# Five reloads on a second queue: which queue starts the first loads of pass two of a scaling kernel

## The chip, the cores and the metric

One core of one Trainium2 chip. In this kernel TensorE sums the pixels, ScalarE helps to pack them and computes the sigmoid, VectorE scales and unpacks, SyncE only starts transfers, and 16 DMA engines move the data between DRAM and SBUF, the core's memory on chip. The metric is the device time of one execution in microseconds; a kernel's time is the median of several. The kernel before took 723.08 us (median of 3 runs, 721.25 to 723.49). A ratio below is the mean time of one kernel's fast runs over that of the kernel before's fast runs of the same rounds, so it is not quite the ratio of the medians beside it.

## The reference

Shortened:

```python
# x: 1 x 384 x 384 x 384 bf16, w1d: 1 bf16
g = jnp.einsum("bhwc->bc", x) / (H * W)      # mean of each channel
s = sigmoid(g * w1d[0])                      # k = 1
return x * s[:, None, None, :]
```

x has 113.2 MB; the kernel's tile on chip holds 275 rows of 768 bytes on 128 partitions, 27 MB. So there are two passes: pass one reads x to sum it, pass two reads again what was not kept, scales it and writes 113.2 MB.

## The kernel before

The 147456 pixels are 1152 rows on each of 128 partitions, 768 bytes a row. Of them 785 are "streamed" (read in both passes) and 367 are kept in SBUF over the middle, most in a packed form which VectorE folds in pass one and unfolds in pass two. One big tile, `arena`, holds everything. The host program plans pass two with a model of one DMA queue, and emits the instructions in the order of that plan.

A small scheduler puts a semaphore wait ahead of every instruction for what it depends on. An engine's queue is served in order, so a wait at its head holds all that stands behind it (a hold put into SyncE's queue on purpose, below, cost 13.7 us):

```python
for s in self.steps:
    eng = engines[s.eng]
    waits = [(sem(d), d.rank * (16 if d.dma else 1)) for d in s.waits]
    ...
    for h, v in waits:
        eng.wait_ge(h, v)
    ins = s.emit()
```

All loads and all stores go through SyncE's queue. A load of pass two waits for the store that empties its rows to land; a store waits for VectorE's multiply:

```python
def load(chunk, a, lo, hi):
    r0, n = chunk
    fl.add(
        "SP",
        lambda: nc.sync.dma_start(out=arena[:, a : a + hi - lo, :], in_=view(xf, r0, n)[:, lo:hi, :]),
        writes=rows(a, hi - lo), dma=True,
    )
...
def store(chunk, a, lo, hi):
    r0, n = chunk
    return fl.add(
        "SP",
        lambda: nc.sync.dma_start(out=view(of, r0, n)[:, lo:hi, :], in_=arena[:, a : a + hi - lo, :]),
        reads=rows(a, hi - lo), dma=True,
    )
...
# pass two, the plan: load whatever run of rows is free
if n >= BIG or n == N_STREAM - todo or (ahead < LOW and n >= 8) or ahead < LAST:
    load(STREAMED, a, todo, todo + n)
```

There are 30 such loads in pass two. Unfolding (`fields`) needs scratch rows that must have been stored first, so VectorE too waits for stores.

## Time and profile before

| | |
|---|---|
| span of the profiled run | 721.3 us |
| bytes moved | 303.87 MB, 421 GB/s over the span |
| pass one, 10 to 264 us | 431 GB/s |
| no data between | about 268.1 and 271.8 us |
| pass two, 312 to 600 us | 430 GB/s, DMA share 1.01 |

The prediction below shows the engines' slices, the stretches and SyncE's waits. Two more views of this kernel are needed. First, the page's queues (packets, MB, share of 16 DMA engines' span): q1 is SyncE's, q10 is ScalarE's.

```profile
q1 hardware_dynamic: 18864, 303.67, 98.6%
...
q10 hardware_dynamic: 2, 0.00, 0.0%
```

Second, VectorE in order of time (start, us, line, form; in brackets the idle time before), around the rows of loads 2 to 5:

```profile
299.94 8.09 DVE L441 TENSOR_TENSOR arena<-arena,s_bf 128x4992 bf16<-128x4992 bf16 x3
310.06 1.76 DVE L441 TENSOR_TENSOR arena<-arena,s_bf 128x3072 bf16<-128x3072 bf16 x1 [2.03 <-DMA arena<-in_x_dram]
```

The three multiplies at 299.94 use loads 2, 3 and 4; the one at 310.06 uses load 5 and was held 2.03 us by it.

### The profile page before, as it was taken

How to read it: one execution, taken by the hardware profiler on the slowest of the kernel's cores; microseconds unless marked ns; L12 is line 12 of the kernel's file. 1: busy time of each engine (PE TensorE's matmuls, PEld its weight loads, DVE VectorE, ACT ScalarE, POOL GpSimd, SP SyncE). 2: the span in 40 equal slices, each digit the busy share in tenths (PEclk: the TensorE clock that was granted, in tenths of full speed). 3: DMA queues.
4: the chain of work that ended last, by engine and by line, in shares of the span. 5: the costliest groups of instructions: out<-in, count | busy, mean ns of one | idle time of the engine just before them, and what ended most of it. 6: DMA issues, size and time to landing. Idle time of an engine off the chain costs nothing.

```text
span 721.3 us, 3240 instructions
## 1 busy us (share of the span) xinstructions
PE 214.6 (30%) x1202; PEld 119.2 (17%) x1202; DVE 496.3 (69%) x470; ACT 115.4 (16%) x92; POOL 0.2 (0%) x4
## 2 busy tenths in 40 slices
PE   4677788897987770000000000000000000000000
PEld 2344445554543430000000000000000000000000
DVE  4600004788899819989799999999996992558500
ACT  3600003566677610002000000000000000000000
POOL 0000000000000000000000000000000000000000
PEclk9799999999899995555555555555555555555555
DMA  9999999999999978999999999999999999999997
GB/s 382 429 443 424 425 435 430 431 433 433 424 427 427 428 320 341 425 430 426 403 430 436 428 438 430 429 439 433 432 432 439 423 445 431 432 430 433 435 436 306
DMA packets 18882, 303.87 MB, mean 421 GB/s; under 512 B 2098, under 2 KB 2098, under 8 KB 4658
## 3 DMA queue, kind: packets, MB, share of 16 engines
q1 hardware_dynamic: 18864, 303.67, 98.6%
q8 instruction: 9, 0.15, 0.1%
q14 instruction: 7, 0.06, 0.0%
q10 hardware_dynamic: 2, 0.00, 0.0%
HBM read 190.41 MB, written 113.25 MB: 421 GB/s over the span
## 4 chain that ended last, share of the span: by engine, by line
DMA 55%; DVE 28%; PE 6%; ACT 5%; SPq 0%; issue 0%; another core or an unknown queue 0%; DVEq 0%
DMA arena<-in_x_dram 38%; DVE arena L441 19%; DMA out_dram<-arena 17%; DVE arena L265 6%; PE bank L241 6%; ACT arena L302 5%; DVE arena L271 3%; SPq L235 0%; ACT s_bf L432 0%; SPq L762 0%; DVEq L112 0%; SPq L106 0%
## 5 line engine op out<-in xcount | busy, mean ns | idle before, releaser
L441 DVE TENSOR_TENSOR arena<-arena,s_bf 128x1536 bf16<-128x1536 bf16 (+8 forms) x103 | 242.3, 2391 | 59.0 <-DMA arena<-in_x_dram 42.0
L265 DVE TENSOR_SCALAR arena<-arena 128x1536 uint16<-128x1536 uint16 (+2 forms) x247 | 145.5, 634 | 113.4 <-DMA arena<-in_x_dram 100.8
L241 PE MATMUL bank<-arena,ones 128*128 128x384 bf16 x1152 | 206.5, 341 | 52.7 <-DMA arena<-in_x_dram 52.6
L241 PEld LDWEIGHTS bank<-arena,ones 128*128 128x128 bf16 x1152 | 114.3, 102 | 144.6 <-DMA arena<-in_x_dram 58.7
L271 DVE TENSOR_TENSOR arena<-arena 128x1536 uint16<-128x1536 uint16 (+2 forms) x114 | 121.2, 1063 | 6.7 <-PE bank L241 4.4
L302 ACT ACTIVATE arena<-arena 128x3072 uint16<-128x3072 uint16 (+1 forms) x38 | 102.5, 2698 | 142.3 <-DVE arena L265 142.3
L514 PE MATMUL bank<-odd,ones 128*128 128x1 bf16 x1 | 0.2, 184 | 329.4 <-DVE odd L509 329.4
L514 PEld LDWEIGHTS bank<-odd,ones 128*128 128x128 bf16 x1 | 0.1, 103 | 329.8 <-DVE odd L509 329.8
L375 ACT COPY arena<-bank 128x512 uint32<-128x512 uint32 (+1 forms) x7 | 4.0, 571 | 61.8 <-DMA out_dram<-arena 61.6
L256 PE MATMUL bank<-ones,zeros 128*128 128x384 bf16 x48 | 8.3, 326 | 0.0
L302 ACT ACTIVATION_READ_ACCUMULATOR arena<-arena 128x1 f32 x38 | 7.1, 188 | 0.0
L256 PEld LDWEIGHTS bank<-ones,zeros 128*128 128x128 bf16 x48 | 4.7, 98 | 3.1
L375 ACT COPY bank<-arena 128x512 uint32<-128x512 uint32 (+1 forms) x7 | 3.6, 565 | 0.0
L432 ACT ACTIVATE s_bf<-bank,w_sc 128x384 bf16<-128x384 f32 x1 | 0.6, 581 | 15.4 <-PE bank L241 15.4
L735 ACT ACT_TABLE_LOAD x1 | 1.3, 1283 | 0.7 <-PEq L751 0.7
L332 DVE TENSOR_SCALAR w_sc<-bank 128x1 f32<-128x1 f32 x1 | 0.2, 159 | 1.1 <-PE bank L327 1.1
L322 DVE MEMSET ones<- 128x128 bf16 x1 | 0.2, 165 | 1.0 <-SPq L106 1.0
L327 PE MATMUL bank<-w_bf,ones 1*128 1x1 bf16 x1 | 0.2, 182 | 2.1 <-DMA w_bf<-in_w1d_dram 2.1
L327 PEld LDWEIGHTS bank<-w_bf,ones 1*128 1x128 bf16 x1 | 0.1, 100 | 2.1 <-DMA w_bf<-in_w1d_dram 2.1
L518 DVE CAST odd_i<-bank 128x1 int32<-128x1 f32 x1 | 0.2, 159 | 0.3 <-PE bank L514 0.3
L504 DVE TENSOR_REDUCE worst<-seen 128x1 f32<-128x38 f32 x1 | 0.2, 185 | 0.0
L509 DVE TENSOR_SCALAR odd<-worst 128x1 bf16<-128x1 f32 x1 | 0.2, 156 | 0.0
(5 smaller groups left out, 0.5 us busy)
## 6 DMA issues: line engine op xcount, KB each, us to landing
arena<-in_x_dram SPq DMA_DIRECT2D x15, 4608.0 KB, 33.9
arena<-in_x_dram SPq DMA_DIRECT2D x22, 1248.0 KB, 11.6
out_dram<-arena SPq DMA_DIRECT2D x8, 3072.0 KB, 30.3
arena<-in_x_dram SPq DMA_DIRECT2D x6, 3072.0 KB, 27.3
out_dram<-arena SPq DMA_DIRECT2D x12, 1248.0 KB, 11.8
out_dram<-arena SPq DMA_DIRECT2D x3, 4608.0 KB, 39.8
arena<-in_x_dram SPq DMA_DIRECT2D x3, 4512.0 KB, 37.9
out_dram<-arena SPq DMA_DIRECT2D x3, 4512.0 KB, 27.7
```

Of the source, the lines that this page charges most:

```text
L241: return nc.tensor.matmul(acc, lhsT=ones[:], rhs=arena[:, i, :], start=first, stop=last)
L256: lambda: nc.tensor.matmul(acc, lhsT=zeros[:], rhs=ones[:, None, :].to_broadcast([P, C // P, P]), start=False, stop=False),
L265: lambda: nc.vector.tensor_scalar(out=dst, in0=src, scalar1=s0, scalar2=s1, op0=op0, op1=op1),
L271: "DVE", lambda: nc.vector.tensor_tensor(out=dst, in0=a, in1=b, op=op), reads=reads, writes=writes
L302: lambda: nc.scalar.activation(out=y, in_=y, func=ACTF.Copy, accum_out=seen[:, 2 * k + i : 2 * k + i + 1]),
L322: fl.add("DVE", lambda: nc.vector.memset(ones[:], 1.0), writes=["ones"])
L327: lambda: nc.tensor.matmul(votes, lhsT=ones[0:1, :], rhs=w_bf[0:1, 0:1], start=True, stop=True),
L375: "ACT", lambda: nc.scalar.copy(dst.bitcast(u32), src.bitcast(u32)), reads=reads, writes=writes
L432: lambda: nc.scalar.activation(out=s_bf[:], in_=acc, func=ACTF.Sigmoid, scale=w_sc[:, 0:1]),
L441: lambda: nc.vector.tensor_tensor(out=v, in0=v, in1=s_bf[:, None, :].to_broadcast([P, n, C]), op=Op.mult),
L514: lambda: nc.tensor.matmul(votes, lhsT=ones[:], rhs=odd[:], start=True, stop=True),
L735: nc.scalar.preload_act_table(ACTF.Sigmoid)
```

## The change

The intent: at the start of pass two the queue of SyncE stands at loads that wait for rows. With the first five loads on ScalarE's queue, whose engine has nothing to do then, a load goes out when its rows are free and the stores behind it don't wait.

```diff
-    def load(chunk, a, lo, hi):
+    def load(chunk, a, lo, hi, queue="SP"):
 
         r0, n = chunk
+        start = nc.sync.dma_start if queue == "SP" else nc.scalar.dma_start
         fl.add(
-            "SP",
-            lambda: nc.sync.dma_start(out=arena[:, a : a + hi - lo, :], in_=view(xf, r0, n)[:, lo:hi, :]),
+            queue,
+            lambda: start(out=arena[:, a : a + hi - lo, :], in_=view(xf, r0, n)[:, lo:hi, :]),
             writes=rows(a, hi - lo), dma=True,
         )
...
+    n_loads, N_ASIDE = 0, 5
...
-                load(STREAMED, a, todo, todo + n)
+
+                load(STREAMED, a, todo, todo + n, "ACT" if n_loads < N_ASIDE else "SP")
+                n_loads += 1
```

## The prediction

> **What bounds the kernel now.** I read the page's slices first. The DMA row stands at 9 in all but two of its 40 digits, and no compute engine does. These four lines carry it:
>
> ```profile
> PE   4677788897987770000000000000000000000000
> DVE  4600004788899819989799999999996992558500
> DMA  9999999999999978999999999999999999999997
> GB/s 382 429 443 424 425 435 430 431 433 433 424 427 427 428 320 341 425 430 426 403 430 436 428 438 430 429 439 433 432 432 439 423 445 431 432 430 433 435 436 306
> ```
>
> A digit is 18 us. TensorE works in slices 1 to 15 (pass one: load all, sum, fold some into an archive on chip), VectorE through pass two (scale, unfold, store, reload what was not kept). The DMA engines are full in both, except where the passes meet. So the question is how many bytes the DMA engines move and when they are idle. I then cut the span at the places that the GB/s row marks:
>
> ```profile
> core 0: us, PE busy (x) PEld busy (x) DVE busy (x) ACT busy (x) POOL busy (x), PEclk, DMA share, GB/s
> 0.00:268.00 268.00, 213.14 (x1194) 118.50 (x1195) 138.43 (x193) 110.86 (x84) 0.20 (x4) 0.95 0.99 423
> 268.00:272.00 4.00, 1.32 (x9) 0.59 (x6) 2.02 (x3) 0.58 (x1) 0.00 (x0) 1.00 0.05 20
> 272.00:276.00 4.00, 0.00 (x0) 0.00 (x0) 4.00 (x3) 0.00 (x0) 0.00 (x0) 0.51 0.88 359
> 276.00:282.00 6.00, 0.00 (x0) 0.00 (x0) 6.00 (x3) 0.00 (x0) 0.00 (x0) 0.50 0.93 303
> 282.00:312.00 30.00, 0.00 (x0) 0.00 (x0) 27.87 (x25) 0.00 (x0) 0.00 (x0) 0.50 1.01 428
> 312.00:600.00 288.00, 0.18 (x1) 0.10 (x1) 272.89 (x233) 4.00 (x7) 0.00 (x0) 0.50 1.01 430
> 600.00:718.00 118.00, 0.00 (x0) 0.00 (x0) 45.12 (x14) 0.00 (x0) 0.00 (x0) 0.50 0.99 426
> ```
>
> The last two columns matter: 0.05 of the DMA time and 20 GB/s between 268 and 272 (last sums, sigmoid, first scaling), 359 and 303 GB/s in the ten us after, then 428 to 430 with a share of 1.0 up to the end. From 282 us on nothing but bytes counts. The chain of waits blames DMA for over half of the span too, but it wanders between loads and stores; in a stage whose DMA engines never rest, which wait comes last says little.
>
> The third view is the SyncE queue's own waits from 268 to 311 us, the time of the five loads that the change moves:
>
> ```profile
> engine line waited for: us in total, times, longest us
> SPq L451 <- DVE arena L441: 38.2, 12, 15.3
> SPq L235 <- DMA out_dram<-arena: 8.0, 4, 2.7
> ```
>
> Loads (L235) held the queue for 8.0 us in four waits, each for the store that empties the load's rows. Is anything ready behind them? I took the issues one by one from the trace, with the semaphore increments that mark their landing (us; KB is bytes per partition times 128):
>
> ```
> store 384 KB   issued 271.83  landed 274.20   frees load 1
> store 768 KB   issued 273.50  landed 276.70
> store 768 KB   issued 275.17  landed 279.34
> LOAD1 768 KB   issued 275.60  landed 283.67
> stores of 768, 1248, 1248, 1248, 768 KB issued 276.84, 279.51, 282.18, 284.85, 286.52
>                landed 285.59, 288.57, 291.55, 294.59, 296.36
> LOAD2 1248 KB  issued 288.58  landed 299.35
> LOAD3 1248 KB  issued 291.57  landed 302.27
> LOAD4 1248 KB  issued 294.61  landed 305.25
> store 1152 KB  issued 294.98  landed 308.06
> LOAD5 768 KB   issued 296.38  landed 310.04
> next store     issued 302.72
> ```
>
> **What the Trainium skill says.** "DMA: Bandwidth & Descriptors", section "Issuing engines are not separate DMA queues": transfers started by scalar or sync run on the same 16 DMA engines and interleave, and starting them from several engines "will only save the time on the sequencer it takes to initiate the DMA". Here an issue takes 0.33 to 0.43 us of the queue, against 8 to 14 us to landing, so there is little of it to save. The same page, "Queues, rings and completion order": each DMA engine takes turns between the queues that have work for it, packet by packet. The trace before can't show this: its one busy queue (q1) carries 98.6% and ScalarE's carries two packets. "Perfetto Trace Analysis", section "DMA Instruction — HWDGE (DVE, Sync)": the record of an issue holds the writing of descriptors, not the data movement. The trace agrees (0.33 us recorded, about 10 to landing), so I use landings for the transfers.
>
> **The change part by part.** Bytes, instructions on VectorE, rows, and the program's own plan are untouched: the plan is computed by a model that doesn't know the queue. Five of the DMA issues leave SyncE's sequence for ScalarE's, each keeping its wait for the store that empties its rows.
>
> 1. Issue time. SyncE loses 5 x 0.34 = 1.7 us of issuing, ScalarE gains it. ScalarE does nothing from 269.9 to 331.6 (its next work, copying the archive's bank back, waits for a store and comes 35 us after load 5). SyncE is idle most of the time. Worth 0 us on either.
>
> 2. The waits taken from SyncE's head. Load 1 was free at 274.20 but stood behind a store that waited for VectorE until 275.17, so it gets out 1.4 us earlier. Loads 2, 3, 4 and 5 were issued within 0.03 us of the landing that frees them, so their own queue doesn't start them earlier. Behind load 4 stood one store: its VectorE multiply ends at 294.8 by the timeline, and it went out at 294.98, a loss of 0.2. Behind loads 2, 3 and 5 nothing was ready. So of 8.0 us of waits some 0.2 was in anyone's way.
>
> 3. What an earlier load 1 fills. The first data follow an issue by about 0.9 to 1.3 us (store issued 270.97, data from about 271.9), so load 1's would come from about 275.3. The engines' real starvation is before that: from the packets, idle 0.6 us between 273.5 and 274.5. From 274.5 to 278.5 they are busy. In 276 to 282 they run at 303 GB/s; at 430 the stretch would have moved 6 x 127 = 762 KB more, so 1.8 us is lost there. The packets show why: the end of a store and load 1, queued in time, have packets of 6144 bytes that take 330 to 770 ns where the rest take 234. That is not starvation by the queue[...] (a like spell, about 1 us in sum, is at 345 to 350). Mixing load 1 with stores may hide part of it. I allow 0.4 us of the 1.8, an estimate.
>
> 4. Sharing. From 289 to 310 two queues have work. By equal turns load 2 would land near 296 instead of 299.35, and the stores behind whose landing loads 3 to 5 wait would land 2 to 6 us later (first near 293, next near 299, then 303), so load 5 starts near 303, not 296.4, and lands near 310 again. The sum of the work is as before, the backlog never falls under 5 us, so the engines stay full. VectorE had 2.0 us of idle time before load 5 and may have 2 to 3 here: not on the path.
>
> Sum: 0.0 + 0.0 (0.2 of a store, under backlog) + 0.4 (+ 0.1 of early bytes) = about 0.5 us less, 0.07%. 723.1 - 0.5 = 722.6.
>
> **Rivals.** (a) Freed stores: the queue's head no longer blocks and pass two runs ahead. For it: 8.0 us of load waits. Against: only one store was ready behind, for 0.2 us, and a DMA share of 1.01 from 282. If I misread and all 8.0 us were real, 715 us (-1.1%); still within 2%. (b) Contention: reads and writes mixed by turns run slower than in blocks. For: the slow packets at 277 to 281, where the writing turns to reading. Against: pass two mixes both already and its 430 equals pass one's 431 (10 to 264 us). If the 25 us of two queues lost 10%, +2.5 us: 725.6. (c) Delayed stores free rows later, and VectorE or the DMA engines run dry around 300 to 315. For: later stores by up to 6 us. Against: 7 to 13 us of backlog from issue to landing. If it bites, +2 to +4: 726. (d) The whole of the slow spell is hidden by mixing: -1.8 us: 721.3.
>
> **Range and chances.** The whole loss of pass two against 430 GB/s is about 5.6 us: 2.4 at its start, 1 at 345 to 350, the rest at the end, where the last packets finish unevenly. So no queueing of five loads can give 2% (14.5 us); and the other way, 25 us of mixed work would have to lose more than half its rate. The runs before spread over 2.2 us. So 722.6, range 720.3 to 725.0; faster 1%, same 98%, slower 1%.
>
> **What would show it.** Load 1 issued near 274.2 and landing near 279 to 281; loads 3 to 5 issued later than before; load 2 landing before its older stores' last; ScalarE's queue with about 5.4 MB; DMA share 1.0 and 428 to 430 GB/s from 282 on. Wrong if GB/s between 282 and 312 leaves 420 to 436, or a slice after it drops, or the last store lands over 3 us from 719.2 by the trace.

## The result, and the profile after

722.71 us, median of 6 runs (721.95 to 723.36), against 722.59 for 6 runs of the kernel before (721.25 to 723.49). Ratio 1.0002, 95% interval 0.9989 to 1.0015: the same. The profiled run has a span of 720.2 us, 1.1 less than the profiled run before, which is within the scatter of the timed runs.

The queues of the changed kernel, then its stretches (us busy per engine, granted clock, DMA share and GB/s in the last two columns):

```profile
q1 hardware_dynamic: 18144, 298.26, 96.8%
q10 hardware_dynamic: 722, 5.41, 2.0%
```

```profile
core 0: us, PE busy (x) PEld busy (x) DVE busy (x) ACT busy (x) POOL busy (x), PEclk, DMA share, GB/s
272.00:276.00 4.00, 0.00 (x0) 0.00 (x0) 4.00 (x3) 0.00 (x0) 0.00 (x0) 0.71 0.92 349
276.00:282.00 6.00, 0.00 (x0) 0.00 (x0) 6.00 (x4) 0.00 (x0) 0.00 (x0) 0.50 0.96 313
282.00:312.00 30.00, 0.00 (x0) 0.00 (x0) 26.25 (x23) 0.00 (x0) 0.00 (x0) 0.50 1.01 429
312.00:600.00 288.00, 0.18 (x1) 0.10 (x1) 274.04 (x234) 4.00 (x7) 0.00 (x0) 0.50 1.01 432
```

5.41 MB have moved to q10. From 272 to 282 us the engines moved 4 x 349 + 6 x 313 = 3274 KB, before 4 x 359 + 6 x 303 = 3254: the start of pass two is as slow as it was. (Counted from 268 us the changed kernel is 120 KB ahead at 282, but its first store also went out 0.23 us earlier, at 270.73 for 270.96, which at 430 GB/s is 99 KB.) From 282 on they are full, at 429 and 432 GB/s.

What waits in SyncE's queue between 268 and 311 us, and the issues on ScalarE's queue (start, us from the first to the last, count):

```profile
SPq L452 <- DVE arena L442: 49.8, 13, 15.2
```

```profile
273.99 0.36 ACTq L236 DMA_DIRECT2D arena<-in_x_dram  x1
```

```profile
286.84 13.30 ACTq L236 DMA_DIRECT2D arena<-in_x_dram  x4
```

The 8.0 us of waits for rows are gone from SyncE's queue. Its waits for VectorE grew from 38.2 to 49.8 us: what it no longer spends at a load it spends at the next store. Next to nothing was ready behind: the one store that stood ready behind load 4 left at 294.62 instead of 294.98.

The issues one by one, put together from the trace as in the prediction (us):

```
                 before                  after
             issued   landed         issued   landed
LOAD1        275.60   283.67         273.99   280.37
store 1248   279.51   288.57         279.28   286.82   frees load 2
store 1248   282.18   291.55         281.95   289.80   frees load 3
store 1248   284.85   294.59         284.61   294.99   frees load 4
store  768   286.52   296.36         286.28   299.78   frees load 5
LOAD2        288.58   299.35         286.84   296.42
LOAD3        291.57   302.27         289.82   301.61
LOAD4        294.61   305.25         295.01   306.69
store 1152   294.98   308.06         294.62   305.54
LOAD5        296.38   310.04         299.80   311.52
next store   302.72   313.04         302.49   311.31
```

Transfers changed places, and at 311 us the two kernels are level. VectorE with the same multiplies as before:

```profile
299.71 5.42 DVE L442 TENSOR_TENSOR arena<-arena,s_bf 128x4992 bf16<-128x4992 bf16 x2
306.70 2.76 DVE L442 TENSOR_TENSOR arena<-arena,s_bf 128x4992 bf16<-128x4992 bf16 x1 [1.57 <-DMA arena<-in_x_dram]
311.54 1.76 DVE L442 TENSOR_TENSOR arena<-arena,s_bf 128x3072 bf16<-128x3072 bf16 x1 [2.08 <-DMA arena<-in_x_dram]
```

It now waits twice, 1.57 and 2.08 us, where it waited 2.03 before. It isn't on the path, since the DMA engines had work throughout.

### The profile page after: what moved, and what is told of

Its sections match the earlier page's. It is cut to its first block, busy times and chain, and to the rows that moved or that the text cites. A ratio compares the mean times of both kernels' runs of the same rounds, so it can differ in the third digit from the quotient of the medians.

```text
span 720.2 us, 3243 instructions
## 1 busy us (share of the span) xinstructions
PE 216.1 (30%) x1202; PEld 119.7 (17%) x1202; DVE 496.0 (69%) x470; ACT 115.4 (16%) x92; POOL 0.2 (0%) x4
## 3 DMA queue, kind: packets, MB, share of 16 engines
q10 hardware_dynamic: 722, 5.41, 2.0%
## 4 chain that ended last, share of the span: by engine, by line
DMA 57%; DVE 29%; PE 5%; ACT 2%; SPq 0%; issue 0%; another core or an unknown queue 0%; DVEq 0%
DMA arena<-in_x_dram 41%; DVE arena L442 20%; DMA out_dram<-arena 16%; DVE arena L266 5%; PE bank L242 5%; DVE arena L272 3%; ACT arena L303 2%; SPq L236 0%; ACT s_bf L433 0%; DVEq L112 0%; SPq L766 0%; SPq L106 0%
```

## The experiments

The theory: from 276 us on the DMA engines always have a transfer waiting, so which queue starts it only changes the order. Its main rival: two effects of some us cancel, a gain from freed waits and a loss from two queues taking turns. Changes are against the kernel after, or before where said.

**Load 1 alone aside.**

```diff
-    n_loads, N_ASIDE = 0, 5
+    n_loads, N_ASIDE = 0, 1
```

> Only load 1 goes through ScalarE's queue; loads 2 to 5 stay on SyncE's. My theory (the DMA engines are full from 276 us on, so order and queue don't matter): within 0.3% of before, load 1 issued near 274.0 and landed near 280.4 as in the changed kernel, loads 2 to 5 issued and landed as in before within 0.5 us. Rival (two effects cancel: load 1's earlier start gains, the taking of turns among loads 2 to 5 and the stores loses): this run has the gain alone and is faster by 1 to 3 us (0.15 to 0.4%), with 282 to 312 us above 430 GB/s.

722.91 us against 722.43, ratio 1.0006 (0.9993 to 1.0019): at most 0.5 us faster. Load 1 went out at 274.28, and the stretches are

```profile
272.00:276.00 4.00, 0.00 (x0) 0.00 (x0) 4.00 (x3) 0.00 (x0) 0.00 (x0) 0.50 0.89 357
276.00:282.00 6.00, 0.00 (x0) 0.00 (x0) 6.00 (x3) 0.00 (x0) 0.00 (x0) 0.50 0.98 309
282.00:292.00 10.00, 0.00 (x0) 0.00 (x0) 9.96 (x11) 0.00 (x0) 0.00 (x0) 0.50 1.02 431
```

The early start of load 1 is worth nothing that these runs can see; the gain of 1 to 3 us that the rival needs isn't there.

**All 30 loads aside.**

```diff
-    n_loads, N_ASIDE = 0, 5
+    n_loads, N_ASIDE = 0, 1000
```

> All loads of pass two go through ScalarE's queue, all stores through SyncE's, so some 145 us of waits for rows leave SyncE's queue and loads and stores take turns for 440 us in place of 25. My theory: within 0.5% of before, 428 to 433 GB/s from 312 to 600 us, stores landing later and loads sooner after issue. Rival 1 (taking turns costs throughput, hidden in the change because it was short): at 2% less throughput over 440 us, 9 us slower. Rival 2 (the waits at the head of SyncE's queue do hold stores back): faster by 3 us or more.

728.23 us against 722.43, ratio 1.0078 (1.0062 to 1.0094): slower by 0.8%, outside what my theory allowed, and the other way from rival 2. So "the queue doesn't matter" holds for five loads and not for thirty. The GB/s row shows where:

```profile
GB/s 379 442 424 428 447 419 430 432 432 432 424 426 427 426 290 373 427 432 421 425 429 396 430 437 412 425 441 430 434 430 434 431 360 415 434 415 435 439 437 352
```

Most slices of pass two are as before; 396, 412, 360 and 415 are holes, in slices of 18 us. Loss in proportion to the turns (rival 1) would lower all of them. The deepest hole, first of this kernel, then of the kernel before:

```profile
586.00:590.00 4.00, 0.00 (x0) 0.00 (x0) 4.00 (x2) 0.00 (x0) 0.00 (x0) 0.50 0.56 163
596.00:600.00 4.00, 0.00 (x0) 0.00 (x0) 4.00 (x2) 0.00 (x0) 0.00 (x0) 0.50 0.94 304
```

```profile
586.00:590.00 4.00, 0.00 (x0) 0.00 (x0) 3.96 (x7) 0.00 (x0) 0.00 (x0) 0.50 1.00 433
```

At 586 to 590 the DMA share is 0.56: the engines are dry (fewer than four of the 16 at work for 2.1 us). At 596 to 600 it is 0.94 at 304 GB/s: busy, but slow. These are two different losses, and the rest of the experiments takes them one at a time. The six runs fall into two groups, three from 726.5 to 727.3 us and three from 729.2 to 729.4. The profiled one, 727.27, is of the first, so what the second group lost besides is in no trace.

**A hold on SyncE, and the same hold on ScalarE.** Both against the kernel before. After the sigmoid ScalarE copies a PSUM tile onto itself 34 times; ahead of the third store stands a 2-byte load that waits for the last copy, in one queue or the other. Both edits in one, shortened:

```diff
+    for _ in range(34):
+        dummy = fl.add("ACT", lambda: nc.scalar.copy(acc, acc), reads=["bank0"], writes=["bank0"])
     def store(chunk, a, lo, hi):
         r0, n = chunk
+        if n_stores[0] == 2:
+            fl.add("SP", lambda: nc.sync.dma_start(out=w_bf[:], in_=w1d.to_broadcast((1, 1))),   # or "ACT", nc.scalar
+                   writes=["w_bf"], dma=True, after=(dummy,))
+        n_stores[0] += 1
```

> A 2-byte transfer that waits for 34 idle ScalarE copies (0.58 us each, about 20 us, so until about 290 us) is put into SyncE's queue after the second store of pass two; all else as in before. My theory: a wait at the head of a queue costs when the DMA engines run dry behind it. They have data until about 274 us and start again about 1.3 us after 290, so about 17 us idle: 14 to 19 us slower (2.0 to 2.6%), DMA share near 0 from 276 to 290. Rival (the program has slack that takes up such a hold, so blocking a queue is harmless in general): under 5 us slower.

> The same 34 copies and the same 2-byte transfer waiting for them, but in ScalarE's queue, which has nothing behind it then. My theory: within 0.3% of before, so the cost in the run with the block on SyncE is the hold itself and not the copies. Rival (the copies or the extra transfer cost by themselves): slower by 3 us or more.

On SyncE: 736.39 us against 722.43, ratio 1.0190 (1.0175 to 1.0205), 13.7 us slower by the ratio (0.019 x 722.4). On ScalarE: 723.06, ratio 1.0014 (0.9997 to 1.0031). The copies took 0.46 us each and 16.8 us together, not 0.58 and 20, so the hold ended at 287 and not at 290; the cost is just under the 14 to 19 us that I expected. The stretch of the kernel with the hold on SyncE, and ScalarE's instructions of the other one:

```profile
276.00:288.00 12.00, 0.00 (x0) 0.00 (x0) 8.85 (x4) 10.14 (x22) 0.00 (x0) 0.50 0.00 0
```

```profile
269.94 16.80 ACT L439 COPY bank<-bank 128x384 f32<-128x384 f32 x34
286.76 0.21 ACTq L456 DMA_DIRECT2D w_bf<-in_w1d_dram  x1
```

From the packets fewer than four of the 16 engines work from 273.9 to 288.1 us, 14.2 us, of which the kernel before has 0.5 too (273.8 to 274.3): 13.7 us more, and 13.7 us slower. So time is lost one for one when the engines are dry, and the same hold on a queue with nothing behind it costs nothing measurable. That is the yardstick for the change: the waits it took from SyncE's head were real, 8.0 us, and no DMA engine was dry because of them.

**Loads 2 to 5 aside, load 1 not.**

```diff
-"ACT" if n_loads < N_ASIDE else "SP"
+"ACT" if 1 <= n_loads < N_ASIDE else "SP"
```

> Loads 2 to 5 go through ScalarE's queue, load 1 stays on SyncE's: the complement of the run with load 1 alone. My theory: within 0.3% of before; load 5 issued near 300 and landed near 311 as in the changed kernel, DMA share 1.0 from 282 to 312. Rival (taking turns of these four costs 1 to 3 us that load 1 earns back): slower by 1 us or more, with GB/s below 425 from 282 to 312.

724.68 us against 722.53, ratio 1.0025 (1.0011 to 1.0038): slower by 1.8 us: inside my 0.3%, but clearly more than no change, and by as much as the rival said. But not where it said: the first line is the time of the turns, the second what follows.

```profile
282.00:312.00 30.00, 0.00 (x0) 0.00 (x0) 26.11 (x23) 0.00 (x0) 0.00 (x0) 0.50 1.01 428
312.00:332.00 20.00, 0.00 (x0) 0.00 (x0) 18.37 (x16) 0.00 (x0) 0.00 (x0) 0.50 1.01 394
```

428 GB/s while the queues take turns, then 394 at a DMA share of 1.01. The packets show a slow spell again, about 1.7 us of excess (time over what packets of that size take elsewhere, summed and divided by 16 engines) from 315 to 326 us, when loads 6 and 7 had just been issued, 0.5 us apart. It is not of loads alone: 0.55 us of the excess lie in the 128 packets of 6144 bytes of the store issued at 315.35, the last before these loads; the rest is in packets of 9984 bytes, the loads' size.

**The first 20 loads aside.**

```diff
-    n_loads, N_ASIDE = 0, 5
+    n_loads, N_ASIDE = 0, 20
```

> The first 20 of the 30 loads of pass two (those up to about 450 us) go through ScalarE's queue. The run with all 30 lost 5.8 us: about 2.5 with the DMA engines dry near 588 us, the rest in spells of slow load packets at 382 to 388, 450 to 455, 590 and 598. My theory for that (stores that take turns with loads land later, free rows and scratch later, until the engines run dry where the backlog is short): this run has no dry stretch after 500 us, and loses only what slow spells or a dry stretch before 500 cost, 0 to 3 us. Rival (throughput is lost in proportion to the number of loads aside): 20/30 of 5.8, about 3.9 us slower, spread evenly with GB/s below 428 in most slices to 450 us.

726.18 us against 722.53, ratio 1.0048 (1.0035 to 1.0062), 3.5 us slower. By the total alone the rival's 3.9 fits and my 0 to 3 doesn't. By place mine fits: next to nothing is lost after 500 us, and before that the excess sits in 380 to 390 (1.1 us) and 445 to 460 (1.45 us), all of it in load packets by their queue. The stretch around 448 is slow, too, but hardly dry: fewer than four engines were at work for 0.07 us only:

```profile
448.00:452.00 4.00, 0.00 (x0) 0.00 (x0) 4.00 (x3) 0.00 (x0) 0.00 (x0) 0.50 0.93 325
```

**The last 10 loads aside.**

```diff
-"ACT" if n_loads < N_ASIDE else "SP"
+"ACT" if n_loads >= 20 else "SP"
```

> The last 10 of the 30 loads (from about 448 us on) go through ScalarE's queue, the first 20 stay on SyncE's. With all 30 aside the DMA engines were dry for about 2 us near 588 and had slow load packets at 590 and 598; with the first 20 aside nothing of that came after 500. My theory (the stretch is made on the spot: the two stores before it take turns with two loads, land later, and VectorE, which needs their scratch rows, has no store ready): dry near 588 again, GB/s under 300 in 586 to 590, in all 2 to 4 us slower. Rival (it is a delay that the first 20 had built up): no dry stretch near 588, and under 1 us slower.

726.84 us against 722.73, ratio 1.0051 (1.0037 to 1.0065), 3.7 us slower. The dry stretch is back in its place (2.0 us with fewer than four engines at work), so ten loads make it on the spot, and no delay from the first twenty is needed. A loss of like size comes with it: 1.8 us of excess in the load packets from 584 to 600 us.

```profile
586.00:590.00 4.00, 0.00 (x0) 0.00 (x0) 4.00 (x2) 0.00 (x0) 0.00 (x0) 0.50 0.55 161
```

How turns make the engines dry: what VectorE's unfolding waited for between 540 and 720 us, in this kernel and in the kernel before.

```profile
DVE arena L266 <- DMA out_dram<-arena: 21.4, 1, 21.4
```

```profile
DVE arena L265 <- DMA out_dram<-arena: 6.2, 1, 6.2
```

21.4 us for a store to land against 6.2. With turns, two loads of 4.6 and 4.7 MB overtook that store (the first was issued at 529.40, 6.9 us after the store, and landed at 550.90, 20.7 us before it); the store was issued at 522.49 and landed at 571.65, in the kernel before at 515.53 and 549.46. Its rows are scratch for the unfolding, so VectorE began at 571.7, and its next store went out at 594.93; in the kernel before two stores went out at 572.75 and 582.55. The next load waited for a store that landed at 587.99. From the end of that store's data (587.65) to the first data of this load (588.98) there was nothing to move in either queue. The loads that came early weren't needed early.

**What makes load packets slow?** Most packets of 6144 bytes take 234 ns. Of load 1's 128 in the changed kernel 47 do, 57 take 330 to 770, and the longest 1004; in the store just before it, too, some are slow (up to 446, 0.27 us of the 1.56 us of excess). The hold on SyncE moved load 1 (issued 288.1, landed 296.0), and the spell went with it (packets of up to 913 ns at 290 to 294), so it isn't the drop of TensorE's clock at 272 us. Two more, both against the kernel before (edits shortened): load 1 and load 5 swap their places in memory; and four small copies from DRAM to DRAM ahead of load 1 are meant to put the DMA engines out of step.

```diff
+        if pass_two and chunk == STREAMED:          # in load and in store
+            by = 47 if hi <= 8 else -47 if 47 <= lo < 55 else 0
+            lo, hi = lo + by, hi + by
```

```diff
+                if todo == 0:
+                    for p in (8, 4, 2, 1):
+                        fl.add("SP", lambda p=p: nc.sync.dma_start(
+                            out=view(of, *STREAMED)[p : 2 * p, 400:408, :],
+                            in_=view(xf, *STREAMED)[p : 2 * p, 400:408, :]), dma=True)   # stored again later, after a wait
                 load(STREAMED, a, todo, todo + n)
```

> As before, on one queue, but load 1 reads (and its rows are stored to) the place in memory of load 5, and the other way about. It asks what makes load 1's packets slow (6144 bytes in 330 to 770 ns, others 234), which the change left as it was. If it is the place in memory: load 5's packets near 305 us are slow and load 1's are 234 ns. If it is the time (first reads after the pause): load 1's packets stay slow near 277 to 281. Time within 0.3% of before either way.

> As before, on one queue, with four small copies ahead of load 1[...] so that the engines don't reach load 1 at the same moment. If the slow spell comes from all engines starting their reads in step, load 1's excess (about 1.3 us in sum before) falls under 0.6 us; if it is the first reads after the pause whatever their order, it stays at 1.2 or more. Time within 0.3% of before, the copies cost under 0.5 us.

Swapped: 722.58 us, ratio 1.0002 (0.9987 to 1.0017); load 1's excess between 274 and 286 us is 1.4 us (before 1.2), load 5 has none. It isn't the place in memory. Staggered: 724.76 us, ratio 1.0028 (1.0013 to 1.0043); the excess stayed at 1.7 us. But this run isn't clean: the fourth copy went as 16 pieces of 384 bytes and not as one packet, the issues of the small copies took 0.56 to 0.99 us each, load 1 went out at 278.80, and fewer than four engines worked from 278.8 to 280.0. The run lost 2 us and not the 0.5 that I wrote. It speaks against engines in step, weakly.

**Load 1 in four parts.** Only load 1 aside, as four transfers of two rows, so that stores come between the parts.

```diff
-                load(STREAMED, a, todo, todo + n, "ACT" if n_loads < N_ASIDE else "SP")
+                if n_loads == 0:
+                    for i in range(0, n, 2):
+                        load(STREAMED, a + i, todo + i, todo + i + 2, "ACT")
+                else:
+                    load(STREAMED, a, todo, todo + n)
```

> Load 1 alone goes through ScalarE's queue, but as four transfers of two rows (192 KB), so that each DMA engine takes turns between a quarter of it and a store. If load packets are slow where all 16 DMA engines only read (what the runs with 20 and 30 loads aside suggest: 4 us lost in the 57 us with 85% or more reading, none where stores are mixed in), the excess of packet time in 275 to 285, 1.6 us with load 1 aside in one piece, falls under 0.8 us; load 1 lands near 284 in place of 280 and VectorE waits under 2 us for it. Time: 0 to 1.5 us faster than the run with load 1 in one piece. Rival (it is the first reads after the pause, mixed or not): the excess stays at 1.3 us or more.

The excess fell from 1.5 us (load 1 in one piece aside) to 0.57, and 276 to 282 us went from 309 to 405 GB/s:

```profile
272.00:276.00 4.00, 0.00 (x0) 0.00 (x0) 4.00 (x3) 0.00 (x0) 0.00 (x0) 0.50 0.80 285
276.00:282.00 6.00, 0.00 (x0) 0.00 (x0) 6.00 (x4) 0.00 (x0) 0.00 (x0) 0.50 1.03 405
```

But 272 to 276 fell to 285 from 357: for 1.3 us from 274.2 the first part's 128 packets of 1536 bytes ran alone. Load 1 was in by 281.4, earlier than I expected, and VectorE didn't wait for it. In all 288 KB more were moved by 282, worth 0.7 us, and the time, 722.62 us against 722.73, ratio 1.0002 (0.9988 to 1.0015), can't show so little. It beats neither kernel. This fits the theory that mixing keeps load packets quick: 0.37 of the 0.57 us lie in the first part, which ran alone, none in the three that followed among the stores; the other 0.20 are in the store beside them. But the packets were also four times smaller and the first part left earlier (273.23 for 274.28), so mixing isn't shown to be the cause by itself. With all 30 loads aside, the queue tells load packets from stores: from 300 to 716 us some 3.7 us of that trace's excess lie in the 55 us in which 85% or more of the packets' time went to loads, and 1.0 us in the other 360. Some 40 of those 55 us ran at full rate, 427 GB/s and more, so loading alone doesn't make a spell.

**Is a slow spell chance?** The changed kernel and the one with loads 2 to 5 aside, again, both on one chip (another than that of the first run of loads 2 to 5).

> The changed kernel once more, beside the one with loads 2 to 5 aside. The latter was 0.25% slower and its trace lost about 1.5 us to slow load packets in 315 to 326, just after two loads that go out together; the changed kernel, with the same two loads together, had none. If such a spell belongs to the program's own timing, the changed kernel shows none between 312 and 330 again and is within 0.15% of before; if it falls by chance, it may show one anywhere and the times of the two programs come together.

> Loads 2 to 5 aside once more. If the spell belongs to the program: slow again in 315 to 326 with 1 to 2 us lost, and 0.15 to 0.4% slower than before. If chance: no spell there, or in another place, and the ratio near 1.000.

The changed kernel: 723.17 us against 722.65, ratio 1.0007 (0.9996 to 1.0019). Loads 2 to 5: 724.61, ratio 1.0025 (1.0013 to 1.0038), the same ratio as the first time. 312 to 332 us of the one and of the other:

```profile
312.00:332.00 20.00, 0.00 (x0) 0.00 (x0) 19.93 (x17) 1.74 (x3) 0.00 (x0) 0.50 1.02 431
```

```profile
312.00:332.00 20.00, 0.00 (x0) 0.00 (x0) 18.40 (x16) 0.00 (x0) 0.00 (x0) 0.50 1.00 389
```

431 against 389 GB/s, and 434 against 394 in their first profiles: the spell belongs to the program. Both have a DMA share of 1.0, so this is rate, not want of work.

## Why the prediction was right

**The bound.** Right: the DMA engines are full from 282 us on, before and after (428 and 429, 430 and 432 GB/s), and the hold on SyncE shows that time is lost when they are dry and then one for one (13.7 us more of it, 13.7 us slower). The last store landed at 718.37 us, within the 3 us of 719.2 that were allowed. A slip in the reading: three of the 40 digits of the DMA row are under 9, not two.

**Steps 1 and 2, issue time and head of the queue.** Right. Load 1 went out at 273.99 (near 274.2 was said), ScalarE's five issues cost nothing, SyncE's freed 8.0 us became waits for VectorE.

**Step 3, 0.4 us from an earlier load 1.** This term failed: nothing was hidden. The excess of slow packets from 274 to 286 us was 1.2 us before and 1.6 after, and the bytes moved from 272 to 282 differ by 20 KB, 0.05 us. (The packets were read too narrowly as well: before the change 5 of the 80 slow ones took over 770 ns, the longest 1455.) I had thought that two queues would mix load 1 with a store packet by packet. They did not: all 128 of load 1's packets, 8 for each DMA engine, started between 276 and 279.6, and no packet of the store issued 0.95 us after it before 279. Load 1 read alone. (On the one queue before, the trace can't tell its packets from the stores'.) Cut in four it was mixed, and the slowness shrank. This was the only gain of note in the sum, so that the total came out near 722.6 is no credit to it: measured was +0.1 us (-0.8 to +1.1), and noise of that size can't tell a gain of 0.5 from none.

**Step 4, turns.** The mechanism was right, the sizes were half right. Load 2 landed at 296.42 (296 was said) and load 5 at 311.52 (310). But the stores before loads 3, 4 and 5 landed at 289.80, 294.99 and 299.78, not 293, 299 and 303, and load 3 went out 1.8 us earlier than before, where "later" was said: load 2's data began only at 290, 3.2 us after its issue, after what the engines had taken up of the other queue. So load 5 started at 299.80 and not at 303. VectorE's waits came to 3.65 us (2 to 3 were said). The work was neither more nor less, as said.

**The rivals.** (a), freed stores: refuted by SyncE's waits and by load 1 alone. (b), turns that run slower: refuted as put, 428 to 429 GB/s in 282 to 312 in every run with four or five aside, and with 30 aside about 1.0 us of excess in the 360 us of mixed stretches. (c), later stores that make the engines dry: absent with five loads, but real: 30 loads and the last 10 alone cost a dry stretch of 2.1 and 2.0 us; the first 20 had next to none (0.07 us) and lost their time to slow packets. The prediction had the mechanism among its rivals and was right that 5 us and more of backlog keep it away here. (d), the slow spell hidden: no.

**What stays open.** Load 1 alone is +0.4 us, loads 2 to 5 are +1.8, all five +0.1 and +0.5: these don't add up, since a slow spell came with one order of loads and stores and not with another. So some cancelling there was, of under 1 us: the spell at 345 to 350 us, 0.94 us of excess in the trace before, is 0.11 in the changed kernel and 0.12 in its repeat, while the start grew by 0.3; over all of pass two the excess is 2.4 us before and 2.3 after. Why engines that only load are slow in some stretches and not in others (pass one does nothing else at 431 GB/s, and 591 to 595 us with 30 loads aside was at full rate) isn't settled. For load 1's spell neither the place in memory nor TensorE's clock is the cause. That spells take in the end of the store before (load 1, and loads 6 and 7) leaves the turn from writing to reading as a rival to loading alone; no run here separates the two.

## What to carry to other kernels

In these runs a wait at the head of a DMA queue cost time only where something ready stood behind it and the DMA engines ran dry meanwhile; read both from the trace before moving work to a second queue. A second queue is also a change of order: loads that go out when their rows are free overtake stores that somebody needs, so be slow to give it all loads. Where the DMA engines are full, look instead for stretches in which they are dry or slow. Putting stores among the loads there may help, but the one try of it (load 1 in four) gained 0.7 us by the trace and nothing that the times can show.

## What the Trainium skill lacked or had wrong

- "DMA: Bandwidth & Descriptors", section "Issuing engines are not separate DMA queues", says that a second issuing engine saves only the time to start a transfer. With five loads that held (ratio 1.0002). It lacks that the order changes with it: the last 10 loads aside cost 0.5%, all 30 cost 0.8%, in part by a stretch with the DMA share at 0.55 and 0.56 where it was 1.00.
- The same page, "Queues, rings and completion order", has an engine drain a whole packet, about 9 to 17 descriptors, from one ring before it turns to the next. The trace after agrees, if 8 data descriptors for each DMA engine and the completion make one such packet: 128 load packets in a row. What the profile counts as packets is finer than these turns.
- No page has that DMA engines which only load can fall to 304 GB/s with a share of 0.94 (596 to 600 us, 30 loads aside) where mixed stretches keep 428 to 430, though pass one, loads alone, keeps 431. The spell at 315 to 326 us came in the same place in both runs of its program.
- No page has a time for the issue of a transfer that comes close behind others. Where it came alone, one on 128 partitions took 0.33 to 0.35 us in pass two of the kernel before; with the hold on SyncE, where eight came in a row, the fourth to the eighth took 0.75 to 1.25 us, and the last of load 1's four parts 1.59. The four small copies, 0.56 to 0.99 us, came in such a row too, so their size and shape need not be the cause.
